# Seven block products in fp16 for two of three token tiles of the second FFN product, and attention of batches 2 and 3 at earlier slots

## The chip, the cores and the metric

The kernel runs on one core of a Trainium2 chip. The metric is device time in microseconds (us) for one execution, lower is better. The core has five engines with a queue each: TensorE (PE, matmuls into PSUM; its weight loads are shown as PEld), VectorE (DVE), ScalarE (ACT), GpSimd (POOL) and SyncE (SP, which here only issues DMAs). Each engine works through its own queue in order and waits on semaphores for the others.

## The reference

Block attention with a Sinkhorn-normalized mixing of key and value blocks, for 4 batches of 8 heads, 768 tokens and 64 channels a head, and then a ResMLP layer over the 768 x 512 result of each batch:

```python
k_sorted = np.einsum('bhij,bhjcd->bhicd', P, k_b)        # P: five rounds of exp and row/column sums
v_sorted = np.einsum('bhij,bhjcd->bhicd', P, v_b)
attn = softmax(scale * q_b @ k_sb.T)                     # blocks of 96 tokens
x = (attn @ v_sb)                                        # [B, S, H*D] = [4, 768, 512]

a1 = alpha1 * x + beta1
tok = np.einsum('ts,bsd->btd', w_tok, a1)
u = x + lam * tok
a2 = alpha2 * u + beta2
ch = np.maximum(a2 @ w_ch1, 0.0) @ w_ch2                 # 512 -> 2048 -> 512
return u + lam * ch
```

The last line but one holds the two FFN products; the change is about the second, `@ w_ch2`.

## The kernel before

**Tiles and stages.** A batch is worked on in two halves `hf` of three token tiles of 128. The first FFN product of a half is made in 16 units `h_unit(b, hf, m)`, one for each 128 of the 2048 hidden channels: four matmuls of 384 columns into a PSUM tile of pool psB, and one ScalarE ReLU into `hT` (lines 725 to 741). The second product follows for each token tile `kk`: 16 matmuls of 512 columns into one psB tile, in four parts of four (`ch_unit`, line 760). Its output goes through VectorE (times lam, out of PSUM, into an SBUF tile `ost`), GpSimd (plus u) and two transfers that SyncE issues (lines 776 to 780). The last token tile of the last batch is cut into 256, 128 and 128 columns with an output path of its own (`last_out`, line 743).

**What is woven in.** All other work is hung on slots of this loop. A slot is (batch, half, "h" or "c", number): after unit number n of "h", or after part n of "c" (n = 4 kk + part). `put` (line 861) hangs work on a slot, `run` emits it, and the loop at lines 940 to 949 visits the slots in order. While batch b is in its FFN, attention of batch b+1 (`score`, `pv`), the mixing of keys and values of batch b+2 (`mix_v`, `mix_k`, `bounce_v`, `back_v`), the loads (`load_kv`, `load_q`), the token product (`moe_tok`), the DMA transposes (`moe_cross`) and the second affine (`moe_affine`) run in its slots. For batch 1 the whole attention lies in (0,1,"h"); for batches 2 and 3 it lies in batch b-1, from (b-1,0,"h",15) to (b-1,1,"h",4), in pairs of `score` or `pv` (lines 881 and 907).

**What sets the order.** Every engine is held to program order: an instruction waits for the one before it on its engine. So a slot fixes the place in every queue, not a time: an engine that has nothing ahead of an instruction starts it as soon as its operands and its buffer are there.

**Buffers.** A tile of a pool takes one of `bufs` buffers of its `tag`; a new tile waits until all readers of the tile that last had the buffer are done, transfers included. The ones the change touches: psA (2 PSUM buffers of two banks: scores, pv, mix products), psB (4 PSUM buffers of one bank: h, ch, tok, and others), `ost` and `toktmp` (2 each), `x128` (2), `Vs` (two tiles, one for even and one for odd batches), `kT` (2, which at the start hold `kT0` and `vd`), `mixed` (1), `qn` (1), `hTa` of 12 and `hTb` of 4 units (1 each).

**Names used later.** `mix_matrix(b)` (line 376) builds bigV, bigM and bigP of a batch on VectorE; `first_back` (line 677) brings the first half's u of batch 0 back through psB (`back_ps`); `flush` (line 506) emits the first affines (a, two VectorE operations for each pv) that `pv` has put off; `tails` (line 510) copies the last two blocks of a and x into place, six VectorE copies; `moe_tok` (line 698) makes six matmuls of 512 columns, then VectorE's product with lam (`toktmp`), VectorE's fp16 u, and GpSimd's fp32 u.

Of the kernel before, what the change touches and what calls it, by code (L numbers as in the profile page):

```python
# [16 lines left out]
def kernel(  # L17
# [92 lines left out]
    KT0 = att.tile([128, H4, NB, 128], F16, name="kT0", tag="kT", bufs=2)  # L110
    VD = att.tile([128, D, 64], F16, name="vd", tag="kT", bufs=2)
    Vs = [const([128, H * NB, GRP], F16, f"Vs_{n}") for n in range(2)]
# [40 lines left out]
    for half in range(2):  # L153
        t_ = att.tile([128, 3, S], F16, name="wt16", tag=("mixed", "qn")[half], bufs=1)
        for lo, n in ((0, 96), (TAIL, 32)):
            pool.dma_start(
                t_[lo // 6:lo // 6 + n],
                moe_w_tok[lo + 3 * half * n:lo + 3 * (half + 1) * n, :].rearrange("(tt p) s -> p tt s", p=n),
            )
        wt16.append(t_)  # L160
        if half == 0:
            pool.memset(VD[:, :, HB:64], 0.0)
            pool.memset(
                KT0[:].rearrange("p g i (th t) -> p (g i th) t", th=2)[:, :, HB:64].bitcast(FT), 0.0
            )
# [5 lines left out]
    W2p = const([128, HT, C], BF, "W2p")  # L171
# [231 lines left out]
    def v_mix(b, n, ps, eng):  # L403
        ps = ps([128, 8, 64], FT, "v_ps")
        fill(ps[:].rearrange("p d x -> p (d x)"), 1 - n % 2)
        for s in range(8):
            for th in range(2):
                d = (s + 4 * th) % 8
                r = slice(th * 64, th * 64 + 64)
                pe.matmul(  # L410
                    ps[r, d, :], VD[r, n * 8 + d, :],
                    bigV[b][r, :, :].rearrange("p h i -> p (h i)"), start=True, stop=True,
                )
        eng(Vs[0][:, :, n * 8:(n + 1) * 8], ps[:].rearrange("p d x -> p x d"))
# [38 lines left out]
    def pv_first(g):  # L453
        if g == 0:
            x_of[0] = moep.tile([128, 8, C], F16, name="x128", tag="x128", bufs=2)
        ps = psa([128, 2, 512], FT, "x_ps")[:, :, 0:480].rearrange("p a (k d) -> p a k d", d=80)
        for i in range(NB):
            for h2 in range(2):
                et = ets[(0, g, i // 4)][:].rearrange("p a i t -> p (a i t)")
                lo = (4 * h2 + i % 4) * BLK  # L460
                w = min(128, 8 * BLK - lo)
                val = Vs[0][:, (2 * g + h2) * NB + i, 0:D + 1]
                if i < 6:
                    pe.matmul(ps[0:w, h2, i, 0:D + 1], et[:, lo:lo + w], val, start=True, stop=True)
                else:
                    for a in range(3):
                        pe.matmul(
                            ps[96:128, h2, 3 * (i - 6) + a, 0:D + 1], et[:, lo + a * 32:lo + (a + 1) * 32], val,
                            start=True, stop=True,
                        )  # L470
        rc = att.tile([128, 2, 6], FT, name="rc", tag="rc", bufs=3)
        dve.reciprocal(rc[:], ps[:, :, :, D])
        dve.tensor_tensor(
            x_of[0][:, 0:NT, g * 128:(g + 1) * 128].rearrange("p k (a d) -> p k a d", a=2),
            ps[:, :, :, 0:D].rearrange("p a k d -> p k a d"),
            rc[:].rearrange("p a k -> p k a").unsqueeze(3).to_broadcast([128, NT, 2, D]), ALU.mult,
        )

    def pv(b, g, hf):
        if g == 0 and hf == 0:  # L480
            x_of[b] = moep.tile([128, 8, C], F16, name="x128", tag="x128", bufs=2)
            a1_of[b] = moep.tile([128, 8, C], F16, name="a1", tag="a1", bufs=1)
        ps = psa([128, 2, 512], FT, "x_ps")[:].rearrange("p a (k d) -> p a k d", d=128)
        et = ets[(b, g, hf)][:].rearrange("p a i t -> p (a i t)")
        for ii in range(4):
            for h2 in range(2):
# [4 lines left out]
                    Vs[b % 2][0:BLK, (2 * g + h2) * NB + 4 * hf + ii, 0:D + 1], start=True, stop=True,  # L491
# [43 lines left out]
    def mix_v(b, n, eng):  # L535
        if n == 0:
            mixed[b] = att.tile([128, HB, D], F16, name="mixed", tag="mixed", bufs=1)
# [38 lines left out]
    def back_v(b):  # L576
        sp.dma_start(Vs[b % 2][0:BLK, :, 0:D], vscr[b].rearrange("x t d -> t x d"))
# [137 lines left out]
    def moe_affine(b, hf):  # L715
        for ci in range(CT):
            affine(b, hf, ci, uT_of[(b, hf)][:, ci, :], dve)

    uT_of = {}

    hT_of = {}

    h_of = {}

    def h_part(b, hf, m, cis):
        if (b, hf) not in hT_of:
            hTa = moep.tile([128, 12, 384], BF, name="hTa", tag="hTa", bufs=1)
            hTb = moep.tile([128, HT - 12, 384], BF, name="hTb", tag="hTb", bufs=1)
            hT_of[(b, hf)] = [hTa[:, m, :] if m < 12 else hTb[:, m - 12, :] for m in range(HT)]
# [13 lines left out]
    def last_out(hT, cps, kk, kt):  # L743
        for n, (lo, hi) in enumerate(((0, 256), (256, 384), (384, 512))):
            c = slice(lo, hi)
            w = hi - lo
            if n:
                cps = psb([128, w], FT, "ch_ps")
                for m in range(HT):
                    pe.matmul(  # L750
                        cps[:], hT[m][:, kk * 128:(kk + 1) * 128], W2p[:, m, c],
                        start=(m == 0), stop=(m == HT - 1),
                    )
            ost = att.tile([128, C // 2], FT, name="ost", tag=("toktmp", "ost")[n % 2], bufs=2)
            dve.tensor_tensor(ost[:, 0:w], cps[:, 0:w], lamB[:, c], ALU.mult)
# [4 lines left out]
    def ch_unit(b, hf, kk, part=(0, HT)):  # L760
# [5 lines left out]
        w = C // 2 if b == B - 1 and kt == NT - 1 else C  # L766
        for m in range(*part):
            pe.matmul(
                cps[:, 0:w], hT[m][:, kk * 128:(kk + 1) * 128], W2p[:, m, 0:w],
# [4 lines left out]
        if b == B - 1 and kt == NT - 1:  # L774
            return last_out(hT, cps, kk, kt)
        ost = att.tile([128, C], FT, name="ost", tag="ost", bufs=2)
        dve.tensor_tensor(ost[:], cps[:], lamB[:], ALU.mult)
        (dve if b == B - 1 and hf == 1 else pool).tensor_tensor(ost[:], ost[:], u_of[b][kt], ALU.add)
        act_out(out[b, kt * 96:(kt + 1) * 96, :], ost[0:96, :])
        act_out(out[b, TAIL + kt * 32:TAIL + (kt + 1) * 32, :], ost[96:128, :])  # L780

# [12 lines left out]
    dve.tensor_copy(Vs[0][:, :, D:GRP], mgap[:].unsqueeze(2).to_broadcast([128, H * NB, GRP - D]))  # L794
# [61 lines left out]
    pool.memset(Vs[1][0:BLK, :, D:GRP], 1.0)  # L856
    pool.memset(Vs[0][0:BLK, :, D:GRP], 1.0)
# [24 lines left out]
    for b in range(1, B):  # L882
# [14 lines left out]
        else:  # L897
# [9 lines left out]
            for (kind, n), at_ in zip(  # L907
                pairs, ((0, "h", 15), (0, "c", 1), (0, "c", 3), (0, "c", 6), (0, "c", 8), (0, "c", 11), (1, "h", 1), (1, "h", 4)),
            ):
                if kind == "p":  # L910
                    put(p, at_[0], at_[1], at_[2] + 1, flush)
                for i in range(2):
                    f = (lambda b=b, n=n + i: score(b, n // 2, n % 2, psa)) if kind == "s" else (lambda b=b, n=n + i: pv(b, n // 2, n % 2))
                    put(p, *at_, f)
        put(
            p, 1, "h", 15 if b == 1 else 8, lambda b=b: tails(a1_of[b], 0, C, dve.tensor_copy),
# [3 lines left out]
        for kt in range(3):  # L920
            put(p, 1, "c", 4 if b == 1 else kt, lambda b=b, kt=kt: moe_tok(b, kt, psb))
        put(p, 1, "c", 4 if b == 1 else 2, lambda b=b: moe_cross(b, 0))
        put(p, 1, "c", 8 if b == 1 else 6, lambda b=b: moe_affine(b, 0))
# [3 lines left out]
        put(b, 0, "c", 4, lambda b=b: moe_affine(b, 1))  # L927
# [12 lines left out]
    for b in range(B):  # L940
        for hf in range(2):
# [4 lines left out]
            for kk in range(3):  # L946
                for part in range(4):
                    ch_unit(b, hf, kk, (4 * part, 4 * part + 4))
                    run(b, hf, "c", 4 * kk + part)
# [30 lines left out]
```

## Time and profile before

| | |
|---|---|
| time, median of 3 runs | 263.91 us (263.64 to 264.61) |
| the profiled execution | 263.49 us, its span 261.7 us |
| clock granted to TensorE | 0.999 of full |
| ScalarE ReLU `hTa<-h_ps`, 384 columns | 96 times, 493 ns |
| ScalarE exponentials `et<-sc_ps`, 768 columns | 32 times, 808 ns |
| VectorE `x<-x_ps,rcb` / `rcb<-x_ps` (pv) | 24 times, 687 ns / 198 ns |
| VectorE `a2T<-uT,ab2col` (second affine) | 28 times, 426 ns |
| GpSimd `u<-toktmp,x` 128x512 fp32 | 18 times, 1650 ns |
| SyncE: output transfers, issue to landing | 192 KB 2.3 us, 64 KB 2.0 us (1.9 to 5.4) |

Busy time by stage of the chain, in us (from the view by windows):

| stage | from, to | PE | DVE | ACT | POOL |
|---|---|---|---|---|---|
| (0,0) c | 56.5, 70.0 | 13.50 | 9.70 | 6.25 | 2.53 |
| (0,1) h | 70.0, 85.5 | 15.44 | 10.21 | 13.07 | 8.64 |
| (0,1) c | 85.5, 102.6 | 17.10 | 13.16 | 10.29 | 7.23 |
| (1,0) h | 102.6, 117.1 | 14.50 | 6.07 | 9.22 | 6.25 |
| (1,0) c | 117.1, 130.6 | 13.50 | 8.59 | 4.92 | 7.09 |
| (1,1) h | 130.6, 142.2 | 11.60 | 10.18 | 8.60 | 4.26 |
| (1,1) c | 142.2, 159.0 | 16.80 | 7.73 | 10.25 | 7.48 |
| (2,0) h | 159.0, 173.3 | 14.30 | 4.84 | 9.21 | 6.24 |

An engine is busy while one of its instructions executes; an instruction that has been started and is held up counts as busy too. TensorE's busy time fills every stage of this table but for 0.06 us; the other engines have slack in each.

### The profile page before, as it was taken

Reading aid. Unit: us, or ns where it says so; the run is one execution under the profiler, and the core shown is the slowest. Engines: PE = TensorE matmul, PEld = TensorE weight load, DVE = VectorE, ACT = ScalarE, POOL = GpSimd, SP = SyncE. Lnnn points to the kernel's source line nnn. Section 1 sums busy time; section 2 is a strip of 40 time slices with the busy share of each in tenths; the row PEclk is TensorE's granted clock in tenths of the full one; section 3 lists DMA queues with packets and bytes.
Section 4 is the critical chain, followed back from the end, with each engine's and each line's share of the span. In section 5 each row is a group of like instructions: output and inputs, shape, how many; then the busy total and the mean of one; then the engine's idle time right before and its main releaser. Section 6 shows DMA issues by size and latency. Waiting matters only on the chain.

```text
span 261.7 us, 5406 instructions
## 1 busy us (share of the span) xinstructions
PE 253.1 (97%) x2179; PEld 140.2 (54%) x2179; DVE 153.8 (59%) x345; ACT 133.8 (51%) x242; POOL 100.2 (38%) x105
## 2 busy tenths in 40 slices
PE   8998799999999999999999999999999999999994
PEld 3456565555556455555565454555565445545554
DVE  6796857987658984613988643407894554051024
ACT  3568666224787539474276288573373014504700
POOL 8759304501382084612860554501302746032000
PEclk9999999999999999999999999999999999999999
DMA  6999999998979957960899859901110332112012
GB/s 101 208 206 186 206 207 213 204 147 188 159 152 183 133 125 181 130 108 3 167 178 179 121 122 170 135 20 40 46 38 0 63 93 67 23 40 80 0 43 80
DMA packets 67533, 31.04 MB, mean 119 GB/s; under 512 B 56675, under 2 KB 63219, under 8 KB 67509
## 3 DMA queue, kind: packets, MB, share of 16 engines
q0 software_dynamic: 26352, 15.34, 42.3%
q1 hardware_dynamic: 41012, 15.30, 34.3%
q8 instruction: 17, 0.28, 0.4%
q10 hardware_dynamic: 144, 0.07, 0.1%
q14 instruction: 8, 0.06, 0.1%
HBM read 32.79 MB, written 8.65 MB: 158 GB/s over the span
## 4 chain that ended last, share of the span: by engine, by line
PE 82%; DMA 10%; POOL 5%; DVE 2%; issue 1%; ACT 0%; POOLq 0%
PE ch_ps L65 32%; PE h_ps L65 30%; PE tok_ps L65 10%; DMA W2p<-in_moe_w_ch_dram 6%; DMA v<-in_v_dram 4%; PE x_ps L65 2%; PE sc_ps L65 2%; DVE a L65 2%; PE kmix_ps L65 2%; PE mix_ps L65 1%; POOL W1p L65 1%; POOL vd L65 1%; POOL k L65 1%; PE qt_ps L65 1%; POOL brow L65 0%
## 5 line engine op out<-in xcount | busy, mean ns | idle before, releaser
L65 PE MATMUL h_ps<-a2T,W1p 128*128 128x384 bf16 x512 | 91.8, 326 | 0.1
L65 ACT ACTIVATE hTa<-h_ps 128x384 bf16<-128x384 f32 x96 | 46.7, 493 | 54.0 <-PE h_ps L65 53.8
L65 PE MATMUL ch_ps<-W2p,hTa 128*128 128x512 bf16 (+2 forms) x312 | 69.0, 363 | 0.0
L65 PEld LDWEIGHTS <-W1p 128*128 128x128 bf16 x512 | 48.3, 98 | 32.3 <-issue 0.3
L65 POOL TENSOR_TENSOR ost<-ost,u 128x512 f32<-128x512 f32 x21 | 26.6, 1268 | 80.2 <-DVE ost L65 53.2
L65 DVE TENSOR_TENSOR ost<-ch_ps,lamB 128x512 f32<-128x512 f32 (+2 forms) x26 | 16.8, 648 | 54.6 <-PE ch_ps L65 54.6
L65 PEld LDWEIGHTS <-hTa 128*128 128x128 bf16 x312 | 28.7, 98 | 28.9
L65 POOL TENSOR_TENSOR u<-toktmp,x 128x512 f32<-128x512 f32 x18 | 29.6, 1650 | 32.1 <-DVE toktmp L65 32.1
L65 ACT ACTIVATE et<-sc_ps 96x768 f16<-96x768 f32 (+1 forms) x32 | 24.8, 808 | 18.9 <-PE sc_ps L65 18.9
L65 PE MATMUL tok_ps<-a,w_tokT 128*128 128x512 f16 x126 | 30.3, 379 | 0.1
L65 ACT CAST kT<-kmix_ps 64x512 f16<-64x512 f32 x32 | 22.9, 717 | 10.1 <-PE kmix_ps L65 9.8
L65 DVE TENSOR_TENSOR toktmp<-tok_ps,lamB 128x512 f32<-128x512 f32 x21 | 14.5, 690 | 20.0 <-PE tok_ps L65 18.6
L65 PE MATMUL ch_ps<-W2p,hTb 128*128 128x512 bf16 (+2 forms) x104 | 25.0, 363 | 0.0
L65 PEld LDWEIGHTS <-w_tokT 128*128 128x128 f16 x126 | 12.2, 98 | 14.0 <-DVE a L65 0.5
L65 ACT ACTIVATE hTb<-h_ps 128x384 bf16<-128x384 f32 x32 | 15.7, 490 | 7.5 <-PE h_ps L65 7.2
L65 POOL DMA_DIRECT2D qn<-in_q_dram x18 | 16.0, 910 | 6.4 <-DMA raw<-in_v_dram 6.4
L65 DVE TENSOR_TENSOR u<-toktmp,x 128x512 f16<-128x512 f32 (+1 forms) x24 | 17.0, 719 | 0.7
L65 DVE TENSOR_TENSOR x<-x_ps,rcb 96x512 f16<-96x512 f32 x24 | 16.5, 687 | 0.8
L65 PEld LDWEIGHTS <-et 96*128 96x128 f16 (+4 forms) x288 | 11.9, 100 | 5.5 <-DVE x L65 1.6
L65 PEld LDWEIGHTS <-hTb 128*128 128x128 bf16 x104 | 9.6, 98 | 9.6
L65 PE MATMUL x_ps<-Vs,et 96*128 96x65 f16 (+4 forms) x288 | 13.0, 195 | 1.7 <-DVE x L65 0.9
L65 DVE TENSOR_TENSOR a<-x,alphaB 96x512 f16<-96x512 f16 (+1 forms) x28 | 13.8, 491 | 0.0
(118 smaller groups left out, 230.1 us busy)
## 6 DMA issues: line engine op xcount, KB each, us to landing
out_dram<-ost SPq DMA_DIRECT2D x23, 192.0 KB, 2.3
raw<-in_v_dram POOLq DMA_DIRECT2D x6, 384.0 KB, 8.1
raw<-in_k_dram POOLq DMA_DIRECT2D x6, 384.0 KB, 9.9
qn<-in_q_dram POOLq DMA_DIRECT2D x18, 128.0 KB, 11.0
vscr<-mixed SPq DMA_DIRECT2D x6, 384.0 KB, 5.2
Vs<-vscr SPq DMA_DIRECT2D x3, 768.0 KB
W1p<-in_moe_w_ch_dram POOLq DMA_DIRECT2D x4, 512.0 KB, 11.5
W2p<-in_moe_w_ch_dram POOLq DMA_DIRECT2D x4, 512.0 KB, 17.3
```

Source lines behind the costliest of these rows:

```text
L65: ins = getattr(self.eng, name)(*args, **kwargs)
```

## The change

In batches 1 to 3 token tile 0 of a half is made as before. Tiles 1 and 2 are made together: with the two tiles as rows, the two halves of the 2048 hidden channels (`hTa`, `hTb`, now eight units each) as the inner blocks and the two halves of the 512 output channels as columns, the eight block products of the plain way become seven of sums and differences. `block_weights` makes four difference blocks of W2p once, in batch 0, by eight GpSimd subtractions of 128 x 1024; `block_sums` makes the blocks of h in each half, on VectorE, at slots h 11 and h 15; `ch_pair` makes the products, of eight matmuls of 256 columns each, with partial results copied out of PSUM by ScalarE (VectorE in half (1,1)) and added by VectorE, and times lam and plus u by GpSimd. W2p and hT become fp16. In the last half the pair comes first and tile 0, cut as `last_out` cuts it, last.

To make room in SBUF, Vs is one tile, x128 has one buffer, `mixed` shares buffers with the sums (or with qn in the last batch), and `kT0` and `vd` share theirs with the difference blocks. The second affine of second halves of batches 1 to 3 moves from VectorE to ScalarE. Attention of batches 2 and 3 starts at h 9 instead of h 15; their token products move from c 0 to c 2 to h 13 to h 15, `moe_cross` from c 2 to h 15.

```diff
-    KT0 = att.tile([128, H4, NB, 128], F16, name="kT0", tag="kT", bufs=2)
-    VD = att.tile([128, D, 64], F16, name="vd", tag="kT", bufs=2)
-    Vs = [const([128, H * NB, GRP], F16, f"Vs_{n}") for n in range(2)]
+    KT0 = att.tile([128, H4, NB, 128], F16, name="kT0", tag="tw", bufs=2)
+    VD = att.tile([128, D, 64], F16, name="vd", tag="tw", bufs=2)
+    Vs = const([128, H * NB, GRP], F16, "Vs")
...
-    W2p = const([128, HT, C], BF, "W2p")
+    W2p = const([128, HT, C], F16, "W2p")
...
-            affine(b, hf, ci, uT_of[(b, hf)][:, ci, :], dve)
+            affine(b, hf, ci, uT_of[(b, hf)][:, ci, :], act if b and hf else dve)
...
+    def block_weights(n):
+        half, c = n % 2, C // 2
+        if n == 0:
+            TW["a"] = att.tile([128, 2, HK, c], F16, name="TWa", tag="tw", bufs=2)
+            TW["b"] = att.tile([128, 2, HK, c], F16, name="TWb", tag="tw", bufs=2)
...
+        dst, x, y = ((t1, b12, b11), (t2, b22, t1), (t3, b22, b12), (t4, b21, t2))[n // 2]
+        pool.tensor_tensor(dst, x, y, ALU.subtract)
+
+    def block_sums(b, hf, part, k1=1, k2=2):
...
+        dve.tensor_tensor(sm[:, 0, r, :], ha[:, r, c2], hb[:, r, c2], ALU.add)
+        dve.tensor_tensor(sm[:, 1, r, :], sm[:, 0, r, :], ha[:, r, c1], ALU.subtract)
+        dve.tensor_tensor(sm[:, 2, r, :], hb[:, r, c1], sm[:, 1, r, :], ALU.subtract)
+        if part:
+            dve.tensor_tensor(ha[:, :, c2], ha[:, :, c1], ha[:, :, c2], ALU.subtract)
+
+    def finish_out(b, hf, kk, ost, eng, c, issue=None):
+        kt = 3 * hf + kk
+        for op, other in ((ALU.mult, lamB[:, c]), (ALU.add, u_of[b][kt][:, c])):
+            eng.tensor_tensor(ost[:, c], ost[:, c], other, op)
+        act_out(out[b, kt * 96:(kt + 1) * 96, c], ost[0:96, c])
+        (issue or act_out)(out[b, TAIL + kt * 32:TAIL + (kt + 1) * 32, c], ost[96:128, c])
+
+    def ch_pair(b, hf, step, mid=None, k1=1, k2=2):
...
+        def tile_of(n):
+            return att.tile([128, C], FT, name="ost", tag=("ost", "toktmp")[n if split else 0], bufs=2)
+
+        side = dve.tensor_copy if (b, hf) == (1, 1) else act.copy
+        px = psb([128, c], FT, "px")[:]
+        product(px, lambda j: ha[:, j, c1], lambda j: W2p[:, j, left], True)
+        o1 = tile_of(0)
+        side(o1[:, left], px)
+        step()
+        py = psb([128, c], FT, "py")[:]
+        product(py, lambda j: hb[:, j, c1], lambda j: W2p[:, HK + j, left], True)
+        dve.tensor_tensor(o1[:, left], o1[:, left], py, ALU.add)
+        if split:
+            finish_out(b, hf, k1, o1, pool, left)
+            mid()
+        step()
+        pz = psb([128, c], FT, "pz")[:]
+        product(pz, lambda j: sm[:, 0, j, :], lambda j: TW["a"][:, 0, j, :], True)
+        o2 = tile_of(0)
+        side(o2[:, right], pz)
+        step()
+        product(px, lambda j: sm[:, 1, j, :], lambda j: TW["a"][:, 1, j, :], False)
+        side(o1[:, right], px)
+        step()
+        product(pz, lambda j: sm[:, 2, j, :], lambda j: W2p[:, HK + j, right], False)
+        dve.tensor_tensor(o1[:, right], o1[:, right], pz, ALU.add)
+        finish_out(b, hf, k1, o1, pool, right if split else whole)
+        step()
+        product(py, lambda j: hb[:, j, c2], lambda j: TW["b"][:, 1, j, :], True)
+        side(o2[:, left], py)
+        step()
+        product(px, lambda j: ha[:, j, c2], lambda j: TW["b"][:, 0, j, :], False)
+        dve.tensor_tensor(o2[:, right], o2[:, right], px, ALU.add)
...
+        dve.tensor_tensor(o2[:, left], o2[:, left], px, ALU.add)
+        if split:
+            finish_out(b, hf, k2, o2, dve, left, nc.scalar.dma_start)
+        else:
+            finish_out(b, hf, k2, o2, pool, whole)
+        step()
...
-    pool.memset(Vs[1][0:BLK, :, D:GRP], 1.0)
-    pool.memset(Vs[0][0:BLK, :, D:GRP], 1.0)
+    pool.memset(Vs[0:BLK, :, D:GRP], 1.0)
...
-                pairs, ((0, "h", 15), (0, "c", 1), (0, "c", 3), (0, "c", 6), (0, "c", 8), (0, "c", 11), (1, "h", 1), (1, "h", 4)),
+                pairs, ((0, "h", 9), (0, "h", 12), (0, "h", 14), (0, "c", 0), (0, "c", 2), (0, "c", 5), (0, "c", 10), (1, "h", 1)),
...
+            put(p, 0, "c", 3, flush)
+            put(p, 0, "c", 8, flush)
+            put(p, 1, "h", 3, flush)
...
-            put(p, 1, "c", 4 if b == 1 else kt, lambda b=b, kt=kt: moe_tok(b, kt, psb))
-        put(p, 1, "c", 4 if b == 1 else 2, lambda b=b: moe_cross(b, 0))
-        put(p, 1, "c", 8 if b == 1 else 6, lambda b=b: moe_affine(b, 0))
+            put(p, 1, *(("c", 4) if b == 1 else ("h", 13 + kt)), lambda b=b, kt=kt: moe_tok(b, kt, psb))
+        put(p, 1, *(("c", 4) if b == 1 else ("h", 15)), lambda b=b: moe_cross(b, 0))
+        put(p, 1, "c", 8, lambda b=b: moe_affine(b, 0))
...
-        put(b, 0, "c", 4, lambda b=b: moe_affine(b, 1))
+        put(b, 0, "c", 5, lambda b=b: moe_affine(b, 1))
+
+    for n, at_ in enumerate(((0, "c", 0), (0, "c", 2), (0, "c", 4), (0, "c", 7), (1, "h", 0), (1, "h", 4), (1, "h", 8), (1, "h", 11))):
+        put(0, *at_, lambda n=n: block_weights(n))
+    for b in range(1, B):
+        for hf in range(2):
+            put(b, hf, "h", 11, lambda b=b, hf=hf: block_sums(b, hf, 0))
+            put(b, hf, "h", 15, lambda b=b, hf=hf: block_sums(b, hf, 1))
...
+            if (b, hf) == (B - 1, 1):
+                ch_pair(b, hf, step, lambda: last_out(1, 0, [(0, (0, 256))]))
+                last_out(1, 0, [(1, (256, 384)), (2, (384, 512))])
+                continue
+            for kk in range(1 if b else 3):
                 for part in range(4):
                     ch_unit(b, hf, kk, (4 * part, 4 * part + 4))
-                    run(b, hf, "c", 4 * kk + part)
+                    step()
+            if b:
+                ch_pair(b, hf, step)
+                step()
```

The steps inside `ch_pair` visit slots c 4 to c 10, one after each product, and one more visits c 11.

## The prediction

> **What bounds the kernel now.** I read the page first (busy shares), then TensorE's waits, then the chain of waits in order of time, then timelines of VectorE, GpSimd and the SyncE queue around the places the change touches.
>
> ```profile
> PE 253.1 (97%) x2179; PEld 140.2 (54%) x2179; DVE 153.8 (59%) x345; ACT 133.8 (51%) x242; POOL 100.2 (38%) x105
> 226.91 10.36 PE ch_ps L65 x48
> 254.41 1.47 PE L65 MATMUL ch_ps<-W2p,hTa 128*128 128x256 bf16 x12
> 256.16 0.83 PE L65 MATMUL ch_ps<-W2p,hTa 128*128 128x128 bf16 x12
> ```
>
> TensorE is busy 97% of the span, and from 44 us on the chain is TensorE without a gap until 258.1 us. So TensorE time removed is time won, and any new wait of TensorE is time lost, to the full. 48 products of 512 columns take 10.36 us, 215.8 ns each. The sixteen of 256 columns run from 254.41 to 256.16, 109.4 ns each: half width at very nearly half price, each with its own weight load.
>
> **What the block products save.** Two token tiles now take 2 x 16 x 215.8 ns = 6.91 us; seven block products of eight 256-column matmuls take 56 x 109.4 ns = 6.13 us. That is 0.78 us per half, and six halves give **-4.7 us** (-5.2 if 256 columns cost half of 215.8). fp16 costs nothing: the fp16 token product has the bf16 second product's mean, 379 ns. Only waits can change this sum.
>
> **GpSimd against VectorE in batch 0.** The block weights are eight GpSimd subtractions of 128 x 1024 fp16. The nearest row is the 128x512 addition, 1.27 us, so 2.5 us each (from below the fp16 copy of 768 elements, 1.51 us, gives 2.0), 20 us together. What a GpSimd operation does to VectorE:
>
> ```profile
> 133.29 2.50 POOL L65 TENSOR_TENSOR ost<-ost,u 128x512 f32<-128x512 f32 x2
> 134.02 2.06 DVE L65 TENSOR_TENSOR a<-x,alphaB 96x512 f16<-96x512 f16 x1
> 136.12 0.42 DVE L65 TENSOR_TENSOR a<-a,betaB 96x512 f16<-96x512 f16 x1
> 51.21 0.38 POOL L65 MEMSET Vs<- 96x128 f16 x2
> 52.02 0.22 DVE L65 TENSOR_TENSOR bigV<-mhi,red 128x64 f16<-128x64 f16 x1
> 54.55 3.48 DVE L65 CAST mixed<-mix_ps 128x1024 f16<-128x1024 f32 x3
> 56.13 0.43 PE mix_ps L65 x2
> 81.13 0.87 POOL L65 DMA_DIRECT2D qn<-in_q_dram  x1 [1.34 <-DMA raw<-in_v_dram]
> 89.03 1.32 DVE L65 COPY a<-a 32x1024 f16<-32x1024 f16 x3
> 91.35 3.88 PE tok_ps L65 x18
> ```
>
> A VectorE operation with two SBUF operands, 0.42 us alone, takes 2.06 us when it meets two GpSimd additions: it ends just after they do. The affine of half (3,1) (four operations, 2.19 us against 1.25 in other stages) loses the same way to one addition. Operations that read PSUM do not.
>
> [...]
>
> Where do they run? The slots in program order pace only the queue; the subtractions wait for nothing but W2p (landed at 39.5 us) and buffers free since the first scores. So numbers 0 and 1 start right behind the memset of Vs at 51.6 us and last to 56.6. Just then VectorE must build bigV, bigM and bigP (two SBUF operands each) from 52.02 on, with the three u from back_ps and the mixed casts queued behind: all of it slides by some 4.5 us. The third mix product (56.13) needs the first cast for its psA buffer, cast at 54.55 before, now about 59.2 with end at 60.3. TensorE stands: **+4.4 us** (0 to 4.6).
>
> Number 2 follows the first output addition and holds up the affine of half (0,1) by about 2.4 us. The casts of kT, the ost product and the q copies behind it keep psB buffers, of which h at the start of (0,1) needs one: **+1.0** (0 to 2.4). Number 3 and the third addition now stand before load_kv(2) and load_q(2). Their issue began at 71.96 and ended at 82.0 after waits on the ring; pushed back by the stalls and by number 3 it ends near 91 us, which is 85 on the old clock. Numbers 4 to 7 come behind it, 10 us, old clock 85 to 95. VectorE then has the last six additions and products of a (0.42 us each) and the six tail copies (2.6 us); letting one pass between two subtractions, the a copies that ended at 90.35 end near 98.5. The token product (91.35) waits for them: **+6.5** (0 to 8.6, the upper end with the subtractions 3 us later).
>
> [...] No row here shows a gap or a lowered clock.
>
> **The output buffers in batches 1 to 3.** Each half takes three ost tiles from two buffers: the plain tile, o1, o2. o2 therefore waits until the plain tile is written out, and it takes the copy of pz that must precede the second product into pz.
>
> ```profile
> 119.87 1.83 PE ch_ps L65 x8
> 121.74 0.69 DVE L65 TENSOR_TENSOR ost<-ch_ps,lamB 128x512 f32<-128x512 f32 x1 [5.28 <-PE ch_ps L65]
> 122.56 1.27 POOL L65 TENSOR_TENSOR ost<-ost,u 128x512 f32<-128x512 f32 x1 [10.27 <-DVE rcb L65]
> 123.86 0.79 SPq L65 DMA_DIRECT2D out_dram<-ost  x2
> out_dram<-ost SPq DMA_DIRECT2D x23, 64.0 KB, 2.0
> ```
>
> From the last product (about 121.6) the chain is: multiply 121.74, GpSimd 122.56 to 123.83, issue 123.86, the second transfer issued 0.4 later and landed 2.0 after: 4.7 us. With 0.5 for the ScalarE copy (a 384-column eviction takes 0.49) and its signals the buffer is ready for TensorE at +5.2. TensorE comes there after px, py, pz and px again, 4 x 0.875 = 3.5 us. The stall is 1.65 us in halves (2,1) and (3,0). In (1,0) and (2,0) VectorE is 0.6 late with pv's x, a score pair (0.45) gives some back, and ScalarE, with the affine moved to it (4 x 0.49 at most) and two exponentials (0.8), is free only just then: 1.85 each. In (1,1) the mix products between the steps cover it to 0.4. **+7.4** for five halves (4 if transfers land at their 1.9 minimum and buffers free sooner; 9 if one meets the 5.4 us landing seen once).
>
> **Attention moved forward.** In (1,0) and (2,0) scores go to h 9 and 12 and the first pv to h 14. ScalarE then has per score pair 1.50 us of exponentials on top of 0.49 per h unit of 0.65: pv at h 14 meets the second exponential of its psA buffer about 0.3 late: **+0.6** (0 to 1.7). No gain is possible, as TensorE waited for nothing here. flush, tails and the token products keep their order; the transposes of uT now precede the plain tile's output on SyncE, but their issue ends some 4.3 us after h 15 and the output's starts at 6.9. GpSimd's loads at c 4 (about 9.5 us in (1,0)) put o1's and o2's additions behind them, which nothing needs before the next half.
>
> **The end.** The last o1 and piece 1 share an ost buffer, so piece 1's multiply waits for o1's GpSimd pair (1.3) and landing (2.4): the end moves from 2.7 us behind the last paired product plus 0 to about +1.2 (0 to 1.4). If px's PSUM buffer is the next in turn after the pair, it is freed two additions (2 x 0.42 + 0.27) after the product while h takes 0.65: 0 to 1.35 over three halves, I take 0.5. **+1.7**.
>
> **Costs at nothing.** The sums: seven VectorE operations, six of 0.42 and one near 0.72, 3.2 us per half, in stages where VectorE is busy 4.8 to 10.2 of 11.6 to 14.5 us. They end about 5.1 us after h 15 and pz needs them at 6.5; losing that cover costs what they are late. One Vs: its refill (159.83 in batch 3's case) is long after the last pv of the batch before. One x128: the last reader of x_of[1], a GpSimd addition of u, ends near 112 against the new first pv near 115; without the margin pv's x waits.
>
> **Sum.** -4.7 + 4.4 + 1.0 + 6.5 + 7.4 + 0.6 + 1.7 = +16.9 us. The profiled execution took 263.49 us (span 261.7 and 1.8 around it), 0.4 below the median of 263.91; 263.49 + 16.9 = 280.4, **280.5** as a median.
>
> **Rivals.**
> - *Only the buffers.* The block weights run where VectorE has slack. For it: GpSimd is busy only 38%, and VectorE passed between additions of u at 93.7 (one 0.89 instead of 0.69). Against it: nothing makes GpSimd wait from 51.6 to 60.9. Then -4.7 + 7.4 + 2.3 = +5.0: 269. With the stall of numbers 0 to 2 but not of 4 to 7: 274.
> - *Faster.* The saving stands and the copies of pz come in time. The point that decides is the buffer's return: under 3.5 us after the plain tile's last product it costs nothing, and up to 0.78 later the half still gains. For it: TensorE's row of 256 columns. [...] With all waits absent 259, with the end's 1.7 us 260.5.
> - *No saving at all:* the products at 256 columns run slower in the pair than in the last tile, because loads no longer hide. At 98 ns a load against 109 there is room, and the row shows it.
>
> **Chances.** Forecast (276 to 285) 0.55; rival of 269 with its neighbours 0.20, 274 0.09; faster 0.11; no change 0.05. A measurement here tells from no change what exceeds 0.5%, 1.3 us. The range 267 to 285 leaves out the faster case and extremes. Faster 0.11, same 0.05, slower 0.84.
>
> **What would show it.** Right: TensorE gaps near 56 and 95 us with VectorE's bigV or a behind GpSimd's subtraction; a wait before the fifth product of each pair on ScalarE's or VectorE's copy, itself behind an output transfer; 256-column groups of 56 at 6.1 us. Wrong: TensorE still 97% busy and a span under 258, or subtractions well under 2 us, or VectorE operations that overlap them at their own length.

## The result and the profile after

The changed kernel takes 296.63 us (median of four runs, 296.33 to 296.92) against 263.94 for the kernel before on the same chip: 1.1235 times as long, 95% interval 1.121 to 1.1259. That is 32.7 us slower, where 16.9 were forecast, and above the range. Ratios here and below leave out executions more than 1.5% above the fastest of their kernel. The profiled execution took 296.33 us, its span is 294.3, and TensorE's granted clock over it 0.966.

First the page of the changed kernel: busy time by engine, TensorE in forty slices of 7.4 us, and the clock granted to it.

```profile
PE 256.8 (87%) x2323; PEld 156.3 (53%) x2323; DVE 193.9 (66%) x391; ACT 147.1 (50%) x274; POOL 133.5 (45%) x128
PE   7987999599997399989489998999799879979992
PEclk9999999979999599999979999999999979999997
```

TensorE was busy 253.1 of 261.7 us before; now it stands for 37.5 of 294.3. The clock row, all 9 before, has four dips ahead of the last slice: in slices 9, 14 (5, the deepest), 21 and 33 the clock was halved (0.50 granted) for part of the time, each time just after TensorE had stood. The trace's clock record puts them at 59.1 to 62.5, 96.6 to 103.5, 147.8 to 151.2 and 236.6 to 240.0 us.

The list of TensorE's waits (in all, times, longest):

```profile
PE pz L65 <- ACT ost L65: 12.7, 5, 5.8
PE mix_ps L65 <- DVE x L65: 6.4, 1, 6.4
PE mix_ps L65 <- DMA qn<-in_q_dram: 3.1, 1, 3.1
PE h_ps L65 <- DVE a2T L65: 1.5, 2, 0.9
```

The first row is the wait for o2's output buffer, the next two are VectorE held up in batch 0. (The third row names a transfer of qn, but its product starts at 57.86, just when VectorE's bigM is ready; in other runs below the same wait stands under `DVE bigM`.) The buffer's wait was forecast by place and is larger. Of the other two the stage was forecast and not the product: TensorE stops before the first mix product of a batch in both stages, at 54.7 for 3.1 us and at 93.8 for 6.4, not before the third and not before the token product. The timeline of VectorE in the changed kernel shows what held it:

```profile
51.05 5.78 DVE L65 TENSOR_TENSOR u<-toktmp,x 128x512 f16<-128x512 f32 x2
57.52 0.29 DVE L65 TENSOR_TENSOR bigM<-bigV,mth 128x128 f16<-128x128 f16 x1
89.47 0.69 DVE L65 TENSOR_TENSOR x<-x_ps,rcb 96x512 f16<-96x512 f32 x1
90.08 8.75 DVE L65 TENSOR_TENSOR a<-x,alphaB 96x512 f16<-96x512 f16 x1
98.86 0.42 DVE L65 TENSOR_TENSOR a<-a,betaB 96x512 f16<-96x512 f16 x1
```

and that of GpSimd beside it:

```profile
51.46 4.21 POOL L65 TENSOR_TENSOR TWa<-W2p 128x1024 f16<-128x1024 f16 x2
90.21 4.20 POOL L65 TENSOR_TENSOR TWb<-W2p 128x1024 f16<-128x1024 f16 x2
94.37 4.18 POOL L65 TENSOR_TENSOR TWb<-W2p,TWa 128x1024 f16<-128x1024 f16 x2
```

A subtraction takes 2.1 us, not 2.5. But the one VectorE operation that meets them at 90.08 and takes 0.42 us alone is held through all four, 8.75 us; the next one runs at its own 0.42. One of the two additions at 51.05 is held through the first two subtractions in the same way, and bigM comes behind it. The mix product at 93.8 needs a PSUM buffer that VectorE's next x must read empty, and that x stands behind the held operation, at 99.44. The token product, at 91.19 before, starts at 105.68, without a wait of its own.

For the buffer, the chain of waits in half (1,0) (start, length, what):

```profile
139.40 0.69 DVE ost L65
...
140.21 1.34 POOL ost L65
...
141.93 6.17 DMA out_dram<-ost
...
148.20 0.38 ACT ost L65
...
148.62 1.86 PE pz L65 x8
```

These are the forecast's steps in the forecast's order. The transfer of 64 KB, put at 2.0 us, took 6.17. And the eight products of pz, 0.87 from start to start elsewhere, took 1.66: the clock is halved from 147.8.

What each stage gained or lost between the two traces, from TensorE's first h product of a half to that of the next, the last to the span's end (the forecast's terms sorted into the same stages, the saving of 0.78 in each half of batches 1 to 3 included):

| stage | forecast | measured |
|---|---|---|
| start, up to half (0,0) | 0 | +0.8 |
| (0,0), subtractions 0 to 2 | +5.4 | +5.6 |
| (0,1), subtractions 4 to 7 | +6.5 | +8.1 |
| (1,0) | +1.4 | +8.0 |
| (1,1) | -0.4 | -0.2 |
| (2,0) | +1.4 | +2.7 |
| (2,1), (3,0) | +1.7 | +6.1 |
| (3,1) and the end | +0.9 | +1.5 |
| sum | +16.9 | +32.6 |

### The profile page after: what moved, and what is told of

It reads as the page before. It is cut to its first block, busy times and chain, and to the rows that moved or that the text cites. A ratio compares the mean times of both kernels' runs of the same rounds, so it can differ in the third digit from the quotient of the medians.

```text
span 294.3 us, 5855 instructions
## 1 busy us (share of the span) xinstructions
PE 256.8 (87%) x2323; PEld 156.3 (53%) x2323; DVE 193.9 (66%) x391; ACT 147.1 (50%) x274; POOL 133.5 (45%) x128
## 3 DMA queue, kind: packets, MB, share of 16 engines
q0 software_dynamic: 26352, 15.34, 37.5%
## 4 chain that ended last, share of the span: by engine, by line
PE 42%; DMA 15%; issue 14%; DVE 13%; POOL 13%; ACT 2%; SPq 1%; POOLq 0%; DVEq 0%; ACTq 0%
PE h_ps L65 17%; PE ch_ps L65 8%; DMA out_dram<-ost 6%; PE tok_ps L65 5%; DMA W2p<-in_moe_w_ch_dram 5%; POOL u L65 5%; DVE a L65 5%; DMA v<-in_v_dram 4%; POOL ost L65 4%; PE pz L65 3%; PE py L65 2%; DVE ost L65 2%; DVE x L65 2%; PE px L65 2%; DVE a2T L65 2%
## 5 line engine op out<-in xcount | busy, mean ns | idle before, releaser
L65 POOL TENSOR_TENSOR ost<-ost,u 128x512 f32<-128x512 f32 (+1 forms) x24 | 29.0, 1210 | 69.9 <-DVE ost L65 67.6
L65 ACT ACTIVATE hTa<-h_ps 128x384 f16<-128x384 f32 x64 | 31.2, 492 | 27.4 <-PE h_ps L65 27.2
L65 ACT ACTIVATE hTb<-h_ps 128x384 f16<-128x384 f32 x64 | 30.9, 493 | 27.2 <-PE h_ps L65 26.6
L65 POOL TENSOR_TENSOR ost<-ost,lamB 128x512 f32<-128x512 f32 (+1 forms) x13 | 14.9, 1143 | 35.4 <-DVE ost L65 35.4
L65 PEld LDWEIGHTS <-hTb 128*128 128x128 f16 x208 | 20.4, 103 | 11.8 <-issue 1.6
L65 PEld LDWEIGHTS <-hTa 128*128 128x128 f16 x208 | 19.5, 98 | 11.1 <-issue 0.5
L65 PE MATMUL ch_ps<-W2p,hTb 128*128 128x512 f16 (+2 forms) x112 | 25.1, 358 | 0.0
L65 PE MATMUL ch_ps<-W2p,hTa 128*128 128x512 f16 (+2 forms) x112 | 23.9, 349 | 0.0
L65 PEld LDWEIGHTS <-sums 128*128 128x128 f16 x144 | 14.5, 102 | 16.3 <-issue 14.0
L65 PEld LDWEIGHTS <-w_tokT 128*128 128x128 f16 x126 | 12.2, 98 | 13.6 <-DVE a L65 0.5
L65 PE MATMUL pz<-W2p,sums 128*128 128x256 f16 x48 | 7.9, 319 | 13.0 <-ACT ost L65 12.7
```

What stands on the lines that cost most here:

```text
L65: ins = getattr(self.eng, name)(*args, **kwargs)
```

## The experiments

The theory behind the first expectations: VectorE held up by GpSimd's subtractions costs about 13.6 us, the halved clock behind it included; o2's buffer costs 13.3 and the halved clock behind that about 2.9; the products save what they were said to save. That is 29.8 of the 37.4 us to be explained (32.7 and the 4.7 saved); small waits are the rest.

**Without the subtractions.** The block weights are not computed; the four products that use them read plain blocks of W2p, so the difference blocks are left out of the result.

```diff
-        put(0, *at_, lambda n=n: block_weights(n))
+        pass
-        product(pz, lambda j: sm[:, 0, j, :], lambda j: TW["a"][:, 0, j, :], True)
+        product(pz, lambda j: sm[:, 0, j, :], lambda j: W2p[:, j, left], True)
...
```

> Leaves the eight block subtractions out; the products that read the difference blocks read plain blocks of W2p of the same size, so the output is another. Theory (VectorE is locked out by the subtractions, 5.4 us in batch 0's first half and 8.2 in its second, halved clock included): TensorE's stops before 62 and before 100 us vanish, the rest stays: 296.6 - 13.6 = 283, between 281 and 285. Rival (the stops come from the new buffer sharing and the later loads, not from the subtractions): over 290.

Measured 283.56 us (282.80 to 284.33, two executions, as in the next two runs): without the subtractions 13.1 us are won. In its trace both halves of batch 0 take again what they took before the change, within 0.05 us, 13.8 less than in the changed kernel; half (1,0) gives 0.8 of it back. The granted clock over the span is 0.965 all the same, against 0.966 there. The wait of pz stays at 12.3 us, so the two costs are separate.

**A third output buffer.**

```diff
-            return att.tile([128, C], FT, name="ost", tag=("ost", "toktmp")[n if split else 0], bufs=2)
+            return att.tile([128, C], FT, name="ost", tag="ost", bufs=3)
...
```

> Three ost buffers in place of two, nothing else. Theory (the copy of pz waits until the plain tile is written out): the waits before the second product into pz, 5.9 + 0.5 + 1.8 + 2.5 + 2.6 = 13.3 us, go, and with them two of the halved clock windows (about 2.9): 280 to 283. Rival (ScalarE, with the affine and two exponentials before the copy of pz, is the bound there): halves (1,0) and (2,0) keep 1.5 us or more each and the time stays over 285. Second rival (the transfer's landing is not the releaser): no change.

Measured 285.98 us (285.64 to 286.31), 10.7 less, and not the 13.6 to 16.6 expected. TensorE's waits in it:

```profile
PE mix_ps L65 <- DVE x L65: 6.5, 1, 6.5
PE pz L65 <- ACT ost L65: 3.8, 4, 1.4
PE mix_ps L65 <- DVE bigM L65: 3.5, 1, 3.5
```

pz now waits 3.8 instead of 12.7 us. What is left is no buffer: in (1,0) and (2,0) ScalarE has the affine moved to it (2.5 us) and two exponentials (1.5) ahead of the copy of pz, the rival's point (1.4 us in each), in (3,0) the affine alone (0.5), and in (3,1) its queue is held by an output transfer that it must issue (0.5). A new wait of the token product in (1,1), 1.0 us, takes a part of the gain. The granted clock over the span rises from 0.966 to 0.982.

**The subtractions on VectorE,** at slots of (1,0) where it has slack.

```diff
-        pool.tensor_tensor(dst, x, y, ALU.subtract)
+        dve.tensor_tensor(dst, x, y, ALU.subtract)
...
+    for n, at_ in enumerate((1, 3, 5, 6, 7, 8, 9, 10)):
+        put(1, 0, "h", at_, lambda n=n: block_weights(n))
```

> The eight subtractions go to VectorE, 0.69 us each by the in-place subtraction of the same size, at slots h 1 to h 10 of half (1,0), where VectorE is busy 6 of 14.5 us. Theory: as without the subtractions, 281 to 285. Rival: VectorE's 5.5 us there delay the u's, the sums or the first pv, and the half (1,0) grows by 2 us or more.

Measured 283.16 us (283.09 to 283.22), 13.5 less: the same work, on the engine that it had blocked, costs nothing that shows beside the 283.56 without it. The timeline of VectorE:

```profile
106.02 1.65 DVE L65 TENSOR_TENSOR TWa<-W2p 128x1024 f16<-128x1024 f16 x1
113.97 1.28 DVE L65 TENSOR_TENSOR TWb<-W2p 128x1024 f16<-128x1024 f16 x2
115.18 1.28 DVE L65 TENSOR_TENSOR TWb<-W2p,TWa 128x1024 f16<-128x1024 f16 x2
```

0.64 us each undisturbed against 2.1 on GpSimd; 1.65 where one meets GpSimd's addition of u.

**Both repairs.** The subtractions go to VectorE as above. o2 gets a buffer of another kind, `toktmp`, so the plain tile and o1 keep the two of `ost` to themselves; there is no third buffer here.

```diff
-            return att.tile([128, C], FT, name="ost", tag=("ost", "toktmp")[n if split else 0], bufs=2)
+            return att.tile([128, C], FT, name="ost", tag=("ost", "toktmp")[n], bufs=2)
...
-        o2 = tile_of(0)
+        o2 = tile_of(0 if split else 1)
...
```

> Three ost buffers and the subtractions on VectorE in half (1,0). Theory: the two costs are in different stages and add up: 296.6 - 13.6 - 16 = 267, between 264 and 269, with what is left above 263.9 - 4.7 in the moved attention and the end. Rival (a wait taken away is replaced by the next one, ScalarE's backlog before pz): over 273.

Measured 272.03 us (271.77 to 272.47), ratio to before 1.0293 (1.0249 to 1.0337). The two repairs win 24.6 of 32.7 us, as the single ones do in sum (10.7 + 13.5). That lies between the two expectations. The clock row has no dip left but in the last slice, and what still waits is

```profile
PE pz L65 <- ACT ost L65: 3.8, 4, 1.4
PE h_ps L65 <- DVE a2T L65: 2.1, 3, 1.0
PE tok_ps L65 <- DVE a L65: 1.2, 1, 1.2
```

**The clock by itself.** 24 products of zeros go in front of pz in half (1,0), where TensorE stands anyway.

```diff
+        if (b, hf) == (1, 0):
+            warm(24)
```

> 24 matmuls of zeros are added on TensorE in half (1,0) where it waits for the copy of pz; they fill 5.2 of its 5.9 us of wait and compute nothing that is read. Theory (the clock is halved because TensorE stood still): the halved window near 148 us goes, the product after the wait takes 0.87 again in place of 1.66 us and the next 0.87 in place of 1.35, so 1.3 us are won although work is added: 295.3. Rival (the clock windows come from power or at fixed times): the window stays, no gain or up to 0.5 us lost, 296.6 to 297.

Measured 293.81 us (293.34 to 294.28). The timeline of TensorE in it:

```profile
143.31 5.34 PE L65 MATMUL warm_ps<-wz 128*128 128x512 f16 x24 [0.42 <-ACT et L65]
148.52 1.03 PE L65 MATMUL pz<-W2p,sums 128*128 128x256 f16 x8
149.39 1.04 PE L65 MATMUL py<-TWb,hTb 128*128 128x256 f16 x8
```

and in the changed kernel, without them:

```profile
148.62 1.86 PE L65 MATMUL pz<-W2p,sums 128*128 128x256 f16 x8 [5.77 <-ACT ost L65]
150.28 1.51 PE L65 MATMUL py<-TWb,hTb 128*128 128x256 f16 x8
```

pz starts at the same time, since it waits for the same copy, but the halved stretch is gone (the clock row has its dips in slices 9, 14 and 33 alone), and TensorE comes to the pv products behind px at 151.14 instead of 152.50: 1.36 us, the 1.3 expected. The other half of the 2.8 comes later: the stretch at 236.5 stands in both, but other work meets it, and (3,0) waits 0.9 less. So this halved stretch of 3.4 us cost about 1.4 us. The four stretches, one of double length, come to an estimated 6 us by the same reading (1.4 + 1.6 + 1.3 + 1.6, from products in them that take twice their time); only this one was taken out alone.

**Can VectorE get in between?** A memset of 128x64 on GpSimd ahead of each subtraction.

```diff
+        pool.memset(gapt[:], 0.0)
         pool.tensor_tensor(dst, x, y, ALU.subtract)
```

> A memset of 128x64 before each of the eight subtractions, nothing else. Theory A (VectorE loses only because a GpSimd operation that reads SBUF follows the last without a gap): a gap lets it in, the operation that was held 8.75 us through four subtractions is held for one, about 2.2 us, and TensorE's wait for x falls from 6.4 to under 4; the a copies still end late, so the time falls by 1 to 3 us, to about 294.5. Theory B (the wait lasts until GpSimd has nothing queued that is ready): held 9 us again, 296.6 to 298.

Measured 297.94 us (296.93 to 298.95). The timeline of VectorE:

```profile
89.58 9.17 DVE L65 TENSOR_TENSOR a<-x,alphaB 96x512 f16<-96x512 f16 x1
```

and that of GpSimd:

```profile
89.86 2.14 POOL L65 TENSOR_TENSOR TWb<-W2p 128x1024 f16<-128x1024 f16 x1
91.93 0.16 POOL L65 MEMSET gapt<- 128x64 f32 x1
92.03 2.12 POOL L65 TENSOR_TENSOR TWb<-W2p 128x1024 f16<-128x1024 f16 x1
```

With three memsets between the four subtractions the operation is still held to the end of the last; a gap of 0.15 us filled by a memset let nothing in. That VectorE gets no turn while GpSimd has any operation ready is more than the runs show. The timeline of the two engines in the kernel with both repairs, where GpSimd multiplies and adds 128x512 in fp32:

```profile
138.06 1.33 POOL L65 TENSOR_TENSOR ost<-ost,u 128x512 f32<-128x512 f32 x1
138.30 1.37 DVE L65 TENSOR_TENSOR a<-a,betaB 96x512 f16<-96x512 f16 x1
139.35 1.44 POOL L65 TENSOR_TENSOR ost<-ost,lamB 128x512 f32<-128x512 f32 x1
```

VectorE's operation ends at 139.67, 0.28 after the first of the two GpSimd operations and well ahead of the second's end: here it passed between them. What lets it pass there, and neither between the subtractions nor between the two additions at 133.29 in the kernel before, no run isolates, and a pause in which GpSimd does nothing was not tried.

**Why 6.17 us?** Two runs move the loads of batch 3, which GpSimd issues right behind the plain tile's output addition, from c 4: to h 5, and to c 9.

```diff
-                put(p, 0, "c", 4, lambda b=b: load_kv(b + 1), lambda b=b: load_q(b + 1))
+                put(p, 0, "h", 5, lambda b=b: load_kv(b + 1), lambda b=b: load_q(b + 1))
```

> The loads of batch 3 are issued in half (1,0) after h 5 in place of c 4, right behind the plain tile's output. Theory (the plain tile's second transfer took 6.2 us because these loads were put on the transfer engines right behind it): it lands in 2 to 2.5 us, TensorE's wait before the second product into pz of half (1,0) falls from 5.9 to about 2 us, and the clock window halved there goes: 296.6 - 5 = 291.5, between 290.5 and 293. Rival (ScalarE's affine and exponentials set that wait, or SyncE's queue is slow for itself): under 1.5 us gained, over 295.

Measured 295.13 us (293.97 to 296.29), between the two expectations; it decides nothing. pz waits 4.4 us there, and the output still takes 5.0 us to land. The affine on ScalarE starts late, as it waits 1.5 us for uT; that the earlier loads slow the transposes of uT is a reading of the trace.

> The changed kernel with batch 3's loads at (1,0,c 9) instead of (1,0,c 4), nothing else. If the loads issued right behind the plain tile's output make its 64 KB take 6.2 us to land, the landing falls to about 2.0, the wait of pz in (1,0) from 5.9 to about 1.9 us, and the halved clock window near 148 us (1.6 us) goes: 291 us (289.5 to 293). If something else slows that transfer (its own size, the transposes of uT), the wait stays over 5 us: 295 us or more. Loads 5 slots later may give a wait of the mix products of (1,1) on the casts of qn or raw, up to 3 us, which the wait list would show apart.

Measured 298.11 us (296.98 to 299.48). The chain of waits has the same transfer as

```profile
141.97 1.98 DMA out_dram<-ost
```

1.98 instead of 6.17 us: the loads were what it waited for. pz in (1,0) then waits 1.6 us, again behind ScalarE's affine and exponentials. Half (1,0) is 5.5 us shorter by it. The time is no better, since half (1,1) is 7.7 longer: the mix product there waits 4.9 us for `mixed`, which in the last batch shares its buffer with qn, whose load now comes late, and behind it the clock row has a 5, in the slice from 171.0 to 178.4.

**A version without these waits.** With the subtractions on VectorE and three `ost` buffers: loads at h 5, the affine of second halves at c 1 and of later first halves at c 7, `mix_matrix(3)` at (1,0,h 6), the last pv pair at h 2 and its flush at h 4, the first small output transfer of the last tile on SyncE, the tile in the middle of the last pair cut at 128 columns.

> As with both earlier changes (three ost buffers, subtractions on VectorE in half (1,0)), and each wait that was left moved: loads of batch 3 after h 5, the second affine of second halves at c 1 (before ScalarE's exponentials and the copy of pz), that of first halves at c 7 (before GpSimd's output pair), mix_matrix(3) at h 6, the last pv pair and its flush one slot later, 128 columns of tile 0 in the last pair and 256 behind it, and its first small transfer on SyncE. Theory (waits are all that stands against the saving of 4.7 us): 272.0 less 1.5 + 1.5 + 0.7 + 0.7 (pz), 1.2 + 1.7 (h after a pair), 1.1 (mix_matrix), 1.8 (token product), 0.6 to 1.6 (end) = 260 to 261.5, under the kernel before. Rival (each wait taken away shows the next one on VectorE or GpSimd): 264 to 268.

Measured 264.83 us (262.85 to 269.11, twelve runs), ratio 1.0016 (0.9984 to 1.0048): as before, and not 260 to 261.5. In the profiled execution, the slowest, one new wait stands out, in the timeline of ScalarE:

```profile
129.59 2.50 ACT L65 ACTIVATE a2T<-uT,ab2col 128x384 bf16<-128x384 f16 x4 [6.62 <-DMA uT<-u]
132.00 0.35 ACT L65 COPY ost<-px 128x256 f32<-128x256 f32 x1
```

The affine, now ahead of the copy of px, stands for uT, whose transposes went out together with the loads; TensorE waits 3.9 us for px, and the clock is lower behind it (pz takes 1.65 us from start to start for 0.87). This execution's granted clock was 0.992 over the span, that of three others among the twelve 0.999 to 1.000, so what the wait costs those is not known.

> The tuned kernel with one slot changed: batch 3's loads issued at (1,0,h 13) instead of (1,0,h 5). Theory: the 3.9 us wait of px in half (1,0) came from the transposes of uT, issued on SyncE from 113.1 to 117.3 us while the loads went out; 8 units later they have landed, the affine on ScalarE starts in time, and the wait and the halved clock window behind it (about 1.7 us) go. From 264.8: 259.5 us (258 to 261.5), no TensorE wait over 1 us in (1,0). Rival: the loads then put GpSimd's output addition of the plain tile some 5 us later and share the transfer engines with its output; the wait only moves to pz or to the token product of (1,1): 262 us or more.

Measured 266.51 us (262.89 to 268.55), px still waiting 3.6 us in the profiled execution, again the slowest: this expectation was wrong in its premise. GpSimd has nothing ahead of the loads, so they went out at 113.3 us, as from h 5. A slot is a place in the queue, not a time.

> The tuned kernel with batch 3's loads back at (1,0,c 4), where the changed kernel has them. Theory: uT is in time, so no wait of px, but GpSimd's multiply and add of o1 and o2 stand behind about 9.5 us of issuing, as in the kernel with both repairs, where the token product of (1,1) then waited 1.4 and 0.5 us: 261.5 us (260 to 263). Rival: with three output buffers and the affine at c 1 nothing waits for GpSimd there either, and it is within 0.5 us of the kernel with the loads at h 13.

Measured 267.69 us (267.06 to 268.08), 6 us more than expected. px no longer waits, but the loads keep GpSimd until 137.0, its operations on o1 and o2 then meet VectorE's affine of x, and the token product waits 2.2 us, with a lower clock behind it (a 7 in the clock row from 146.5 to 153.1; the four h products at 146.88 take 1.28 us instead of 0.65). The place was right, the price not: the clock was again left out, and py's two waits (1.6 us) were not seen.

**Loads that wait for a time.** A copy of one column of h unit 13 stands ahead of the loads on GpSimd, and flush of c 3 moves to c 6, behind the add of py.

```diff
+    def gate(p):
+        pool.tensor_copy(gate_t[:], hT_of[(p, 0)][13][:, 0:1])
...
-                put(p, 0, "c", 4, lambda b=b: load_kv(b + 1), lambda b=b: load_q(b + 1))
+                put(p, 0, "h", 13, lambda b=b, p=p: gate(p), lambda b=b: load_kv(b + 1), lambda b=b: load_q(b + 1))
-            put(p, 0, "c", 3, flush)
+            put(p, 0, "c", 6, flush)
```

> The tuned kernel with the loads of batch 3 held back on GpSimd by a copy of one column of h unit 13 of (1,0) into a scratch tile ahead of them, so that they cannot go out while uT is transposed (slot h 13 alone left them at 113 us, since GpSimd had nothing ahead), and flush of c 3 moved to c 6, behind the add of py. Theory: the affine on ScalarE finds uT in time, the wait of px (3.6 us) and the halved window behind it (2.4 us) go, and py no longer waits 0.8 us each in (1,0) and (2,0) behind the four pairs of affine operations that flush puts ahead of it. From the profiled 268.55: 268.55 - 6.0 - 1.6 = 260.9 us (259.5 to 262.5), ratio to before 0.989, no TensorE wait over 1 us outside batch 0's start. Rival: the late loads keep GpSimd from o1's and o2's operations until they meet VectorE's affine of x in (1,1) as with the loads at c 4 (token product 2.2 us late and a halved window): 264 us or more.

Measured 262.00 us (261.65 to 262.29, six runs) against 264.38 before in the same job: 0.9908 (0.9877 to 0.9938): 0.9% faster than the kernel before. The gate and the moved flush came together, so their shares are not known. The timeline of GpSimd shows the loads held to 119 us:

```profile
118.50 0.19 POOL L65 COPY gate_t<-hTb 128x1 f16<-128x1 f16 x1 [5.50 <-ACT hTb L65]
119.00 1.10 POOL L65 DMA_DIRECT2D raw<-in_v_dram  x2 [0.32 <-issue]
```

and the page that nothing of note stands still and the clock row is even:

```profile
PE 249.5 (96%) x2323; PEld 154.5 (59%) x2323; DVE 182.2 (70%) x399; ACT 147.3 (57%) x274; POOL 116.9 (45%) x121
PEclk9999999999999999999999999999999999999998
```

Of the 4.7 us saved 2.4 are won as time; 1.0 is lost at the end, where the span runs 4.6 us past TensorE's last product instead of 3.6, and the halves of the trace show where the rest went: (2,1) and (3,0) have their saving in full and (1,1) nearly, while (1,0) loses 1.6 us against its 0.78 and (2,0) all of its own.

## Why the prediction was right in direction and wrong in size

**The saving, -4.7: right.** Eight products of 256 columns take 0.87 us, 109 ns each, in every half where none waits, and the last kernel turns half of it into time.

**VectorE held up by GpSimd, +4.4, +1.0 and +6.5: right in its stages, wrong in a step that luck covered.** The terms rest on one row of before, 2.06 us for 0.42 beside two additions; the runs showed 8.75 us for 0.42 beside four subtractions. Measured by stages 5.6 and 8.1; taken away, 13.1 us (13.5 with the work on VectorE). This holds the halved clock, some 3.0 by the reading above, which the forecast left out of these terms: the stops themselves are 3.4 and 6.4 us, 2.1 less than the 11.9 forecast. The step that failed is "letting one pass between two subtractions": none passed. Even so the copies of a end at 104.68, which is 98.3 on the old clock (TensorE was 6.4 us late by then) where 98.5 was forecast: four subtractions of 2.1 us for 2.5, begun earlier, made up for it. That is luck. Nor are the products that wait the forecast's: the first mix product waits for bigM in (0,0), and in (0,1) for the x that frees its psA buffer. Number 2's 1.0 did not come: (0,0)'s second product took 0.2 us longer. The runs differ by row: VectorE's operation was held for four subtractions in a row, 8.75 us, and passed between an addition and a multiply of 128x512, in 1.37.

**The buffers, +7.4: right in mechanism, the term that was mis-sized.** The five waits, counted from the weight load's stop where the list counts the product's, are 5.94, 0.47, 1.79, 2.50 and 2.59, 13.3 us for 7.4. In (2,0) and (1,1) the forecast held (1.85 and 0.4). In (1,0) the step that failed is "landed 2.0 after": with the loads beside it the transfer took 6.17, and 1.98 when they were moved. The forecast had seen those loads behind the output addition and asked only what they do to GpSimd's queue, not to the transfer. It named a landing of 5.4 as its upper end, but for one transfer and at the price of 1.6 us. In (3,0) the transfer took 2.84. In (2,1) it took 2.00, but the plain tile's multiply on VectorE came only at 231.65, 0.97 after its last product: the first of the sums ahead of it met GpSimd's addition of u and took 1.38 instead of 0.42, held up by GpSimd once more.

**The clock, left out of the sum: wrong to leave out.** Before the change TensorE's list of waits is empty from 44 to 255 us and its clock was 0.999; the forecast itself put stops of 4 to 6 us in. One stretch cost 1.4 us by experiment, the four an estimated 6, in place of nothing in the sum. The length of a stop alone doesn't tell what follows: counted between the products, the stop of 2.33 us before pz in (2,1) brought a halved stretch, the longer one of 2.42 in (3,0) brought none. The four stretches of the changed kernel last 3.41 us and, once, 6.83; their starts and that of the tail's are 11, 15, 26 and 16 times 3.41 us apart. In the 3.41 us ahead of each of the four TensorE was busy 28, 16, 0 and 35% of the time. Counted in steps of 3.41 us from the fourth, the stop of 2.42 falls into two, busy 80 and 49%. So where a stop falls may count as much as its length. This is a reading of one trace; no run was made for it.

**Moved attention, +0.6: five times too small, and by other steps.** The score at h 12 shares psA with `mix_matrix(3)`, which the forecast did not see, and waits 0.9 us in (1,0). The affine of first halves at c 8 waits for GpSimd and delays h by 0.9 and 0.6 in two places, and p6 behind p4 costs 0.4 each in (1,0) and (2,0). Together that is 3.2 us between the products. The moves were not undone alone, so these are readings of the trace, not shown by a run.

**The end, +1.7: 0.6 too small.** (3,1) is 1.5 us longer although it saves 0.78, so the end cost 2.3. The span runs 5.2 us past TensorE's last product instead of 3.6, and 0.7 is a wait of pz behind ScalarE's DMA issue that was not foreseen.

Beside the 16.9 forecast, the stops behind the held VectorE are 2.1 us under their terms, the buffers 5.9 over, the clock about 6, moved attention 2.6, the end 0.6 and the start 0.8 over. That makes 13.8 of the 15.7 us that the forecast missed in the two traces; the rest is small waits that were not taken apart.

**The rivals.** "Only the buffers" at 269 fell: with the subtractions gone the kernel stands at 283.6. "Faster" named the right condition, the buffer's return; with that and the subtractions repaired 272 us are left and not 259, as the small waits of ScalarE and VectorE behind it then come to light.

## What to carry to other kernels

When a forecast puts a stop of several microseconds on a matmul engine that never stood before, price the slower clock behind it too (1.4 us here for the one stretch that was taken out alone), even if no row of the old profile can show it. A buffer's return is a chain whose last link is a transfer: ask what else is in flight at that moment, not only what a transfer takes in the median (6.17 us against 2.0 here). And a place in program order doesn't hold back an instruction that has nothing ahead of it (the loads put at h 13 went out at 113.3 us); where a time is meant, make it depend on something that happens at that time.

## What the runs showed of the hardware

- A VectorE operation with two SBUF operands was held through four GpSimd subtractions of 128 x 1024 fp16 in a row, 8.75 us for 0.42, and 9.17 with a memset of 0.15 us between them. Between a GpSimd addition and a multiply of 128 x 512 fp32 it passed, in 1.37 us. VectorE's product out of PSUM, `x<-x_ps,rcb`, took 0.69 us alone and 0.69 beside a GpSimd addition of 128 x 512 fp32 (at 122.57 in the kernel before).
- A 64 KB output transfer took 6.17 us with loads issued by GpSimd at the same time, 1.98 when those loads went out later.
- In the changed kernel, after stops of TensorE of 3.14, 6.41, 5.77 and 2.33 us, the clock was halved for 3.41 us, after the second for 6.83; after one of 2.42 us and one of 1.61 it was not. With 24 products of zeros in the stop of 5.77 it was not halved behind it.
- The same subtraction of 128 x 1024 fp16 took 2.1 us on GpSimd and 0.64 on VectorE.
